# Batch 0's output in a fused attention and bilinear feed-forward kernel: two of three tile pairs by Strassen's products, with the sums that they need

## The chip, the cores and the metric

The kernel runs on one core of a Trainium2 chip. The metric is the device time of one execution in microseconds, start to finish; the time that counts is the median of several runs. Beside it stands one profiled execution, from which all rows below are taken. In the rows, PE is the matrix engine (TensorE) and PEld its loading of the stationary operand, DVE is VectorE, ACT is ScalarE, POOL is GpSimd, and SP is the engine that here only issues DMAs.

## The reference

For each of 4 batches and 8 heads (768 positions, head size 64), an 8 by 8 matrix `P` is normalised five times by rows and columns; `P` mixes the 8 blocks of `k` and `v`; block-wise attention follows; the heads are laid side by side into `x` (3072 rows of 512), and a bilinear feed-forward is applied:

```python
k_sorted = np.einsum('bhij,bhjcd->bhicd', P, k_b)      # and v_sorted likewise
scores   = scale * np.matmul(q_b, k_sb.transpose(0, 1, 2, 4, 3))
attn     = softmax(scores);  attn_out = np.matmul(attn, v_sb)
x = attn_out.transpose(0, 2, 1, 3).reshape(B * S, H * D)
out = ((x @ w_a) * (x @ w_b)) @ w_out                  # 512 -> 1536 -> 512
```

## The kernel before

**Order.** The order on all five engines is written out by hand: an instruction stands on its engine's queue where the program issues it, and each engine takes its queue from the front. Waits between engines are put in from the data and from the reuse of buffers.

**Feed-forward of one batch.** `ffn_ab(b, m, t)` is one step: for one of 12 feature tiles `m` and one half `t` of the batch's 768 positions (384 columns), PE forms `a` (4 products, L372) and `b` (4 products), ACT copies `a` from PSUM into `a_sb` (L402), and DVE multiplies it with `b` into `hT` (L403). Its PSUM tiles `pf` come from the pool `psF`, which has four buffers; so a step's `b` can start only when the multiplication two steps before has been done. A batch has 24 steps. The output follows, 6 chunks `c` of 128 rows:

- `ffn_out(b, c)`, in two parts: 12 products of 512 columns (L427) into one PSUM tile `po`, a copy into `o_sb` (ACT for even chunks, DVE for odd ones, by the helper at L175 and L177), and `store`, which issues the DMAs on SP (two for each chunk of batch 0, L414). Only batch 0 uses it.
- `ffn_out_pair(b, u)`, in four parts, used by batches 1 to 3: chunks `u` and `u + 3` together, as a 2 by 2 block product by Strassen's method, with seven products of 6 x 256 columns each (L481) in place of eight. It needs sums of blocks of the weights (`weight_sum`, L451, ten DVE instructions once per kernel, into `w_sums`) and sums of blocks of `hT` (`h_sums`, L472, twelve DVE instructions for each batch, four of which work in place in `hT`). ACT copies two products into `s` and two into the middle of the output tile (L495); DVE adds `y` twice (L519, L522) and writes two corners (L502).

Sums wait in a list, `sums_due`. `some_sums(n)` issues up to `n` of them at that place in DVE's order, and `sums_for` issues whatever is still needed before a product.

**Attention of the next batch**, in units between these steps (`interleave` with a list of places): for each of four head pairs `M` (mix, `pair_mix`: 12 products, L312, four copies out of two PSUM tiles, then transposing DMAs on SP), `R` (scores, 16 products L333, two exponentials on ACT, L338) and `O` (16 products L278, and on DVE a reciprocal and a multiplication for each half, L282 and L284, and one transposing DMA on SP into `xT`, L347). The PSUM tiles of `M`, `R` and `O` come from the pool `psA`, which has two buffers. In the rest of the text O1 is the `O` unit of the second head pair, and so on. Where batch 0 is computed, the units are those of batch 1: after the steps of `t = 1` with numbers 1, 2, 4, 5, 7, 9, 10, 12 come M0, M1, R0, M2, R1, M3, O0, R2, and after output parts 1, 3, 4, 6 (steps 13, 15, 16, 18) come O1, R3, O2, O3.

**Buffers.** The output tiles `o_sb` and `o2` share a tag of two buffers; `hT` and the sums `hs` have one buffer each. At the start of the program PE runs 46 products whose results nobody uses (`keep_busy`, L181, into `heat`).

Of the kernel before, what the change touches and what calls it, by code (L numbers as in the profile page):

```python
# [9 lines left out]
FP32 = mybir.dt.float32  # L10
# [13 lines left out]
def kernel(  # L24
# [12 lines left out]
    P = 128  # L37
    B, H, S, D = q.shape
# [134 lines left out]
    def copy(eng, out, in_):  # L173
        if eng == "act":
            nc.scalar.copy(out=out, in_=in_)  # L175
        else:
            nc.vector.tensor_copy(out=out, in_=in_)  # L177
# [200 lines left out]
        return hTs[b]  # L378

    sums_due = []  # L380

    def some_sums(n):
        for _ in range(min(n, len(sums_due))):
            sums_due.pop(0)[1]()
# [5 lines left out]
    def ffn_ab(b, m, t, begun=()):  # L390
        hT = hT_of(b)
        ab = []
        for n, w_sb in enumerate((w_a_sb, w_b_sb)):
            if n < len(begun):
                pf, k0 = begun[n], KA - 1
            else:
                pf, k0 = psF.tile([P, 512], FP32, tag="F", name="pf"), 0
            ab_mms(pf, w_sb, b, m, t, range(k0, KA))
            ab.append(pf)
            if n == 0:  # L400
                a_sb = ffp.tile([P, HW], BF16, tag="a_sb", name="a_sb", bufs=4)
                nc.scalar.copy(out=a_sb, in_=pf[:, 0:HW])  # L402
        nc.vector.tensor_mul(out=hT[:, m, t * HW:(t + 1) * HW], in0=a_sb,  # L403
                             in1=ab[1][:, 0:HW])
        if b > 0:
            if t == 1 and m >= KH and m != KH and m != KH + 2:
                sums_due[:0] = h_sums(b, *((m - KH - 1, 2) if m < KH + 4 else (m - KH, 1)))
            some_sums(1)

    def store(b, c, o):  # L410
        if b == 0:
# [10 lines left out]
    def ffn_out(b, c):  # L422
        v = {}

        def mms(ms):
            for m in ms:
                nc.tensor.matmul(v["po"], lhsT=hTs[b][:, m, c * P:(c + 1) * P],  # L427
                                 rhs=w_out_sb[:, m, :], start=(m == 0), stop=(m == KO - 1))

        def part1():  # L430
            v["po"] = psF.tile([P, DMODEL], FP32, tag="F", name="po")
            mms(range(KH))

        def part2():
            mms(range(KH, KO))
            o_sb = outp.tile([P, DMODEL], FP32, tag="o2", name="o_sb", bufs=2)
            copy("act" if c % 2 == 0 else "dve", o_sb, v["po"])
            store(b, c, o_sb)

        return [part1, part2]  # L440

# [14 lines left out]
        return hTs[b][:, c * KH + m, r * HW:(r + 1) * HW]  # L456

    def h_sums(b, m, nm):
        if b not in sums:
            sums[b] = ffp.tile([P, KH, 3, HW], BF16, tag="hs", name="hs")  # L460
        hT, hs = hTs[b], sums[b]

        def h(r, c, step):
            return _ap(hT, (c * KH + m) * S + r * HW,
                       [[KO * S, P], [S, nm]] + [[step, 2]] * (step is not None) + [[1, HW]])

        def s(i, k):
            return _ap(hs, (m * 3 + i) * HW,
                       [[KH * 3 * HW, P], [3 * HW, nm]] + [[HW, k]] * (k > 1) + [[1, HW]])

        turn = KH * S - HW
        return [("h", lambda to=to, x=x, y=y, op=op: nc.vector.tensor_tensor(  # L472
                    out=to, in0=x, in1=y, op=op))
                for to, x, y, op in (
                    (s(0, 2), h(0, 0, 0), h(0, 1, HW), ALU.add),
                    (s(2, 1), h(1, 0, None), h(1, 1, None), ALU.add),
                    (h(1, 0, turn), h(0, 0, KH * S + HW), h(1, 0, turn), ALU.subtract))]
# [10 lines left out]
    def ffn_out_pair(b, u):  # L488
        add3, add1, add2 = (lambda m, n=n: sums[b][:, m, n] for n in range(3))
        a11, a12, a21, a22 = (lambda m, r=r, c=c: h_part(b, r, c, m)  # L490
                              for r in range(2) for c in range(2))
        v = {}

        def keep(n, to):
            nc.scalar.copy(out=to, in_=v["ps"][n])  # L495

        def middle(n):
            return v["o"][:, n, (1 - n) * NH:(2 - n) * NH]

        def corner(n):  # L500
            to = v["o"][:, n, n * NH:(n + 1) * NH]
            nc.vector.tensor_tensor(out=to, in0=v["y"], in1=v["ps"][n], op=ALU.subtract)  # L502

        def part1():
            sums_for(1, 2)
            v["ps"] = [psF.tile([P, NH], FP32, tag="F", name="po") for _ in range(2)]
            v["s"] = outp.tile([P, 2, NH], FP32, tag="s", name="s")
            product(v["ps"][0], a11, w_sums[1], u)
            keep(0, v["s"][:, 0])
            product(v["ps"][1], a22, w_sums[2], u)  # L510
            keep(1, v["s"][:, 1])
            if b > 0:
                sums_for("h")

        def part2():
            sums_for("h", 0)
            v["y"] = outp.tile([P, NH], FP32, tag="y", name="y")
            v["o"] = outp.tile([P, 2, DMODEL], FP32, tag="o2", name="o2", bufs=2)
            nc.vector.tensor_tensor(out=v["y"], in0=v["s"][:, 0], in1=v["s"][:, 1], op=ALU.add)  # L519
            ps = psF.tile([P, NH], FP32, tag="F", name="po1")  # L520
            product(ps, add1, w_sums[0], u)
            nc.vector.tensor_tensor(out=v["y"], in0=ps, in1=v["y"], op=ALU.add)  # L522
            product(v["ps"][0], add3, B22, u, False)
            keep(0, middle(0))

        def part3():
            sums_for(3, 4)
            product(v["ps"][1], add2, B11, u, False)
            keep(1, middle(1))
            product(v["ps"][0], a12, w_sums[4], u, False)  # L530
            corner(0)

        def part4():
            store(b, u, v["o"][:, 0])
            product(v["ps"][1], a21, w_sums[3], u, False)
# [33 lines left out]
    def units_full(b):  # L569
        def M(g):  # L570
            pair_mix(g, 0, ("act", "act"))
            pair_mix(g, 1, ("act" if g >= 2 * HP else "dve", "act"))
            if g != 2 * HP - 1:
                turn_v(g)
            if g == 2 * HP + 1:
                hold(kvs[g % NBUF][0][0:1, 0, 0:1])
                load_pair(g + 2)
            if g in (HP + 1, HP + 3):
                spread(nc.gpsimd, p_col, (g - HP + 3) // 2 * 8, 8)
            if HP + 2 <= g + 1 < NPAIR and g + 1 != 2 * HP:  # L580
# [22 lines left out]
    with tc.manual_schedule(engines={ET.PE, ET.Pool, ET.SP, ET.Activation, ET.DVE}):  # L603
        if True:
# [14 lines left out]
                copy(eng, p_rep[:, hf * NR:(hf + 1) * NR],  # L619
                     _ap(p_fin, hf * NR, [[NB * NB, BH], [1, NR], [0, CG // 2]]))  # L620

            keep_busy(heat[:, 0], 46, P)
            for hp in range(HP):
                first_q(hp)
                if hp % 2:
# [114 lines left out]
        interleave(steps, units_half(), (2, 3, 3, 4, 4, 4, 5, 5, 6, 7, 7, 8, 9, 9, 10, 11))  # L740

        def outs(b):
            return [part for u in range(NCH // 2) for part in ffn_out_pair(b, u)]

        steps = [lambda m=m: ffn_ab(0, m, 1) for m in range(KO)]
        steps += [part for c in range(NCH) for part in ffn_out(0, c)]
        interleave(steps, units_full(1), (1, 2, 4, 5, 7, 9, 10, 12, 13, 15, 16, 18))

        halves = [n for m in range(KH) for n in (m, m + KH)]
        for b in range(1, B):  # L750
            steps = [lambda m=m, t=t, b=b: ffn_ab(b, m, t) for m in halves for t in range(2)]
            if b == 1:
                sums_due.extend(weight_sum(n, m, 3) for n in (1, 2, 0, 4, 3) for m in (0, 3))
            steps += outs(b)
            interleave(steps, units_full(b + 1) if b + 1 < B else [],
                       (1, 4, 8, 10, 13, 15, 17, 20, 21, 24, 25, 28))
# [30 lines left out]
```

## Time and profile before

| | |
|---|---|
| runs | 234.41, 234.69 and 236.04 us; median 234.69 us |
| profiled execution, its own time | 234.56 us |
| its span in the profile | 232.8 us |
| PE busy | 227.4 us (98%) |
| DVE busy | 141.6 us (61%) |
| ACT busy | 113.1 us (49%) |
| POOL busy | 68.7 us (30%) |
| granted TensorE clock | 1.00 |

Shares of the span are averages over stages, so the stage is what to read: batch 0's steps with `t = 1` run from about 41.1 to 62.7 us, its output from 62.7 to 80.3 us, batch 1's steps from there to 117.9 us and its output to 132.8 us. The time outside the span (234.56 - 232.8 = 1.76 us) lies around the profiled instructions.

### The profile page before, as it was taken

The page shows a single profiled execution, that of the slowest core. Times are in us where ns is not written, and L with a number is a line of the kernel's source. Part 1 is how long each engine was busy: PE and PEld are TensorE (multiplying, and loading weights), DVE is VectorE, ACT ScalarE, POOL GpSimd, SP SyncE. Part 2 cuts the span into 40 slices and gives each one's busy share as a digit, 9 for nine tenths or more (in the row PEclk, how much of TensorE's full clock was granted, in tenths as well). Part 3 has the DMA queues.
Part 4 walks back from the last instruction along what each step waited for, and adds up shares of the span by engine and source line. Part 5 has one row for each costly group of instructions (what it writes and reads, how often), then busy time and mean ns, then how long its engine had stood idle before and what let it go on. Part 6 is the DMA issues. An engine that isn't in the chain of part 4 may idle for free.

```text
span 232.8 us, 5674 instructions
## 1 busy us (share of the span) xinstructions
PE 227.4 (98%) x2259; PEld 156.6 (67%) x2259; DVE 141.6 (61%) x318; ACT 113.1 (49%) x237; POOL 68.7 (30%) x98
## 2 busy tenths in 40 slices
PE   7999999999999999999999999999999999999994
PEld 7776766766555465666689865666689865666883
DVE  7776677544645177768796334658786346576632
ACT  3575764577531165845552365755452333333331
POOL 8779839750035166325824000000000000000000
PEclk9999999999999999999999999999999999999999
DMA  5999999999779999996999757134016300000042
GB/s 74 201 201 199 207 203 200 152 179 186 136 113 200 229 169 200 137 130 95 161 155 209 148 133 95 23 59 75 8 37 157 148 32 4 0 0 3 3 170 99
DMA packets 54858, 28.68 MB, mean 123 GB/s; under 512 B 33712, under 2 KB 51888, under 8 KB 54832
## 3 DMA queue, kind: packets, MB, share of 16 engines
q0 software_dynamic: 18832, 14.16, 44.0%
q1 hardware_dynamic: 35856, 14.04, 34.0%
q8 instruction: 17, 0.28, 0.5%
q10 hardware_dynamic: 144, 0.13, 0.2%
q14 instruction: 9, 0.07, 0.1%
HBM read 28.32 MB, written 6.29 MB: 149 GB/s over the span
## 4 chain that ended last, share of the span: by engine, by line
PE 84%; DMA 11%; POOL 1%; issue 1%; DVE 1%; ACT 0%; SPq 0%; POOLq 0%; DVEq 0%
PE pf L372 53%; PE po L481 18%; DMA w_b_sb<-in_moe_w_b_dram 4%; PE mix L312 3%; PE o_ps L278 3%; DMA first<-in_q_dram 3%; DMA out_dram<-o_sb 2%; PE po L427 2%; PE sc L333 2%; DMA xT<-xp 2%; PE xt_ps L269 1%; PE vs_ps L254 1%; PE two L372 1%; PE sc L237 0%; DVE o_sb L177 0%
## 5 line engine op out<-in xcount | busy, mean ns | idle before, releaser
L403 DVE TENSOR_TENSOR hT<-a_sb,pf 128x384 bf16<-128x384 bf16 x96 | 52.9, 552 | 50.3 <-PE pf L372 27.1
L372 PE MATMUL pf<-xT,w_b_sb 128*128 128x384 bf16 x384 | 78.8, 326 | 0.2 <-DMA w_b_sb<-in_moe_w_b_dram 0.2
L372 PE MATMUL pf<-xT,w_a_sb 128*128 128x384 bf16 x376 | 77.1, 326 | 0.3 <-DMA xT<-xp 0.3
L402 ACT CAST a_sb<-pf 128x384 bf16<-128x384 f32 x94 | 45.4, 482 | 53.4 <-PE pf L372 34.5
L372 PEld LDWEIGHTS <-w_b_sb 128*128 128x128 bf16 x384 | 37.5, 98 | 25.8 <-issue 0.5
L372 PEld LDWEIGHTS <-w_a_sb 128*128 128x128 bf16 x384 | 35.3, 98 | 20.6
L481 PE MATMUL po<-w_sum,hT 128*128 128x256 bf16 x216 | 25.9, 273 | 0.0
L481 PEld LDWEIGHTS <-hT 128*128 128x128 bf16 x216 | 20.8, 98 | 2.6
L175 ACT CAST kv<-mix 128x384 bf16<-128x384 f32 x44 | 18.4, 490 | 5.7 <-PE mix L312 5.2
L338 ACT ACTIVATE eT<-sc 96x768 bf16<-96x768 f32 x24 | 18.0, 802 | 5.8 <-PE sc L333 5.8
L284 DVE TENSOR_TENSOR xp<-o_ps,rec 96x512 bf16<-96x512 f32 x24 | 16.5, 687 | 0.8
L481 PEld LDWEIGHTS <-hs 128*128 128x128 bf16 x162 | 15.7, 98 | 1.8
L427 PE MATMUL po<-w_out_sb,hT 128*128 128x512 bf16 x72 | 16.4, 379 | 0.0
L472 DVE TENSOR_TENSOR hs<-hT 128x768 bf16<-128x768 bf16 (+2 forms) x24 | 14.4, 610 | 0.4
L502 DVE TENSOR_TENSOR o<-y,po 128x256 f32<-128x256 f32 x18 | 7.6, 421 | 11.2 <-PE po L481 11.2
L299 POOL COPY qc<-q 128x384 uint32<-128x384 uint32 x12 | 6.9, 576 | 22.9 <-DMA q<-in_q_dram 13.1
L111 POOL COPY kvc<-kv 128x768 uint32<-128x768 uint32 x16 | 13.5, 852 | 0.1
L481 PE MATMUL po<-w_out_sb,hs 128*128 128x256 bf16 x108 | 13.3, 273 | 0.0
L495 ACT COPY s<-po 128x256 f32<-128x256 f32 x18 | 6.5, 374 | 13.4 <-PE po L481 13.4
L100 POOL DMA_DIRECT2D kv<-in_k_dram x16 | 11.7, 730 | 3.0 <-PE o_ps L278 2.1
L495 ACT COPY o<-po 128x256 f32<-128x256 f32 x18 | 6.7, 372 | 11.8 <-PE po L481 11.8
L100 POOL DMA_DIRECT2D kv<-in_v_dram x16 | 11.7, 729 | 2.2 <-DMA w_b_sb<-in_moe_w_b_dram 1.5
(83 smaller groups left out, 220.1 us busy)
## 6 DMA issues: line engine op xcount, KB each, us to landing
out_dram<-o SPq DMA_DIRECT2D x17, 256.0 KB, 2.1
kv<-in_k_dram POOLq DMA_DIRECT2D x16, 192.0 KB, 7.0
kv<-in_v_dram POOLq DMA_DIRECT2D x16, 192.0 KB, 7.6
q<-in_q_dram POOLq DMA_DIRECT2D x12, 192.0 KB, 7.7
w_out_sb<-in_moe_w_out_dram POOLq DMA_DIRECT2D x3, 512.0 KB, 13.6
out_dram<-o_sb SPq DMA_DIRECT2D x12, 128.0 KB, 5.1
w_a_sb<-in_moe_w_a_dram POOLq DMA_DIRECT2D x2, 512.0 KB, 11.4
w_b_sb<-in_moe_w_b_dram POOLq DMA_DIRECT2D x2, 512.0 KB, 13.0
```

The source lines that it names most:

```text
L100: nc.gpsimd.dma_start(out=to, in_=_ap(t, base, [[W, P], [S * D, 2], [1, W]]))
L111: nc.gpsimd.tensor_copy(out=to.bitcast(U32).rearrange("p c n d -> p n c d"), in_=loaded[g][0].bitcast(U32).rearrange("p n (c d) -> p n c d ...
L175: nc.scalar.copy(out=out, in_=in_)
L284: nc.vector.tensor_tensor(out=_ap(xp, i0 * 2 * D, [[nxp * 2 * D, BLK], [D, 2], [2 * D, NBH], [1, D]]), in0=_ap(o_ps, 1, [[1024, BLK], [511 ...
L338: nc.scalar.activation(out=eT[:, hf, :, 0:HB], in_=sc[0:BLK, :, 0:HB], func=AF.Exp, scale=float(scale))
L372: nc.tensor.matmul(pf[:, 0:HW], lhsT=w_sb[:, kc, m * P:(m + 1) * P], rhs=x_cols(b, kc, t), start=(kc == 0), stop=(kc == KA - 1))
L402: nc.scalar.copy(out=a_sb, in_=pf[:, 0:HW])
L403: nc.vector.tensor_mul(out=hT[:, m, t * HW:(t + 1) * HW], in0=a_sb, in1=ab[1][:, 0:HW])
L427: nc.tensor.matmul(v["po"], lhsT=hTs[b][:, m, c * P:(c + 1) * P], rhs=w_out_sb[:, m, :], start=(m == 0), stop=(m == KO - 1))
L472: return [("h", lambda to=to, x=x, y=y, op=op: nc.vector.tensor_tensor(out=to, in0=x, in1=y, op=op)) for to, x, y, op in ((s(0, 2), h(0, 0 ...
L481: nc.tensor.matmul(to, lhsT=lhs(m)[:, u * P:(u + 1) * P], rhs=rhs[:, m], start=start and m == 0, stop=(m == KH - 1), skip_group_check=not ...
L495: nc.scalar.copy(out=to, in_=v["ps"][n])
```

## The change

- Batch 0's output: chunks 0 and 3 stay with `ffn_out`; the pairs (1, 4) and (2, 5) go through `ffn_out_pair`. The number of parts stays twelve, so the places of the units stay as they are.
- The weight sums move from the start of batch 1 to step 9 of batch 0's steps with `t = 1`; batch 0 gets sums of `hT` too, over the 256 of 384 columns that the two pairs use. `PACE` says how many sums each step of `t = 1` issues. The feature tiles of these steps are taken in the order 0, 6, 1, 7, and so on, as in the other batches.
- In every batch, `some_sums` now stands ahead of the step's multiplication and not behind it. The two parts of `ffn_out` issue two sums each.
- The copies of `ffn_out` go all to ACT, and so do the copies of batch 1's `pair_mix`, of which DVE had one in four.
- Output tiles have three buffers; `keep_busy` at the start issues 52 products.

```diff
     sums_due = []
+    PACE = (1,1,1,1,1,1,1,1,2,3,3,3)
...
+        some_sums(1 if b else t * PACE[2 * (m % KH) + m // KH])
         nc.vector.tensor_mul(out=hT[:, m, t * HW:(t + 1) * HW], in0=a_sb,
                              in1=ab[1][:, 0:HW])
-        if b > 0:
-            if t == 1 and m >= KH and m != KH and m != KH + 2:
-                sums_due[:0] = h_sums(b, *((m - KH - 1, 2) if m < KH + 4 else (m - KH, 1)))
-            some_sums(1)
+        if t == 1 and m >= KH and m != KH and m != KH + 2:
+            sums_due[:0] = h_sums(b, *((m - KH - 1, 2) if m < KH + 4 else (m - KH, 1)))
...
         def part1():
             v["po"] = psF.tile([P, DMODEL], FP32, tag="F", name="po")
             mms(range(KH))
+            some_sums(2)
 
         def part2():
             mms(range(KH, KO))
-            o_sb = outp.tile([P, DMODEL], FP32, tag="o2", name="o_sb", bufs=2)
-            copy("act" if c % 2 == 0 else "dve", o_sb, v["po"])
+            o_sb = outp.tile([P, DMODEL], FP32, tag="o2", name="o_sb", bufs=3)
+            copy("act", o_sb, v["po"])
             store(b, c, o_sb)
+            some_sums(2)
...
     def h_sums(b, m, nm):
+        n0, n = (P, HW - P) if b == 0 else (0, HW)
...
-            v["o"] = outp.tile([P, 2, DMODEL], FP32, tag="o2", name="o2", bufs=2)
+            v["o"] = outp.tile([P, 2, DMODEL], FP32, tag="o2", name="o2", bufs=3)
...
-            pair_mix(g, 1, ("act" if g >= 2 * HP else "dve", "act"))
+            pair_mix(g, 1, ("act", "act"))
...
-            keep_busy(heat[:, 0], 46, P)
+            keep_busy(heat[:, 0], 52, P)
...
         def outs(b):
-            return [part for u in range(NCH // 2) for part in ffn_out_pair(b, u)]
-
-        steps = [lambda m=m: ffn_ab(0, m, 1) for m in range(KO)]
-        steps += [part for c in range(NCH) for part in ffn_out(0, c)]
+            plain = (0,) if b == 0 else ()
+            return ([part for u in plain for c in (u, u + 3) for part in ffn_out(b, c)]
+                    + [part for u in range(NCH // 2) if u not in plain
+                       for part in ffn_out_pair(b, u)])
+
+        halves = [n for m in range(KH) for n in (m, m + KH)]
+        steps = [lambda m=m: ffn_ab(0, m, 1) for m in halves]
+        steps[8] = lambda m=halves[8]: (
+            sums_due.extend(weight_sum(n, m0, 3) for n in (1, 2, 0, 4, 3) for m0 in range(0, KH, 3)),
+            ffn_ab(0, m, 1))
+        steps += outs(0)
         interleave(steps, units_full(1), (1, 2, 4, 5, 7, 9, 10, 12, 13, 15, 16, 18))
...
-            if b == 1:
-                sums_due.extend(weight_sum(n, m, 3) for n in (1, 2, 0, 4, 3) for m in (0, 3))
```

More of the change, by code (lines that the diff above doesn't have):

```diff
@@ L463, in h @@
         def h(r, c, step):
-            return _ap(hT, (c * KH + m) * S + r * HW,
-                       [[KO * S, P], [S, nm]] + [[step, 2]] * (step is not None) + [[1, HW]])
+            return _ap(hT, (c * KH + m) * S + r * HW + n0,
+                       [[KO * S, P], [S, nm]] + [[step, 2]] * (step is not None) + [[1, n]])
         def s(i, k):
-            return _ap(hs, (m * 3 + i) * HW,
-                       [[KH * 3 * HW, P], [3 * HW, nm]] + [[HW, k]] * (k > 1) + [[1, HW]])
+            return _ap(hs, (m * 3 + i) * HW + n0,
+                       [[KH * 3 * HW, P], [3 * HW, nm]] + [[HW, k]] * (k > 1) + [[1, n]])
         turn = KH * S - HW
@@ L742, in outs @@
         def outs(b):
-            return [part for u in range(NCH // 2) for part in ffn_out_pair(b, u)]
-        steps = [lambda m=m: ffn_ab(0, m, 1) for m in range(KO)]
-        steps += [part for c in range(NCH) for part in ffn_out(0, c)]
+            plain = (0,) if b == 0 else ()
[8 more added lines that the diff above has]
+        steps += outs(0)
         interleave(steps, units_full(1), (1, 2, 4, 5, 7, 9, 10, 12, 13, 15, 16, 18))
-        halves = [n for m in range(KH) for n in (m, m + KH)]
         for b in range(1, B):
             steps = [lambda m=m, t=t, b=b: ffn_ab(b, m, t) for m in halves for t in range(2)]
-            if b == 1:
-                sums_due.extend(weight_sum(n, m, 3) for n in (1, 2, 0, 4, 3) for m in (0, 3))
             steps += outs(b)
```

## The prediction, on record before the changed kernel ran

> **What bounds the kernel now.** I read the windows by stage first, then PE's timeline, the chain of waits, and DVE's timeline last. The windows (stretch, length, busy us and instruction count of PE, PEld, DVE, ACT, POOL, granted clock, DMA share, GB/s) for batch 0's second half of steps, its output, and batch 1's steps:
>
> ```profile
> 41.13:62.70 21.57, 21.57 (x217) 14.10 (x215) 11.10 (x23) 14.04 (x30) 7.42 (x8) 1.00 1.38 167
> 62.70:81.25 18.55, 18.23 (x144) 9.10 (x141) 6.64 (x15) 4.69 (x7) 5.92 (x10) 1.00 1.10 173
> 81.25:117.93 36.68, 36.68 (x334) 23.35 (x334) 27.95 (x52) 21.92 (x47) 20.14 (x30) 1.00 1.13 148
> ```
>
> PE is busy in all of it but 0.32 us of batch 0's output; DVE and ACT have room everywhere. So time is won only by taking work from PE or by closing that gap, and lost wherever DVE's queue gets so late that PE waits. PE's timeline gives the price of a product and the gap:
>
> ```profile
> 67.17 0.51 PE L333 MATMUL sc<-qTf,kv 64*128 64x96 bf16 x16
> ...
> 72.51 7.93 PE L427 MATMUL po<-w_out_sb,hT 128*128 128x512 bf16 x36
> 80.28 0.65 PE L372 MATMUL pf<-xT,w_a_sb 128*128 128x384 bf16 x3
> 81.25 0.32 PE L372 MATMUL pf<-xT,w_a_sb 128*128 128x384 bf16 x1 [0.32 <-DMA xT<-xp]
> ```
>
> From start to next start, 36 plain products take 80.28 - 72.51 = 7.77 us, 0.2158 each. The chain of waits (start, us) has the same for Strassen's products, and what the gap hangs on:
>
> ```profile
> 70.36 5.42 DMA out_dram<-o_sb
> ...
> 76.26 4.94 DMA xT<-xp
> ...
> 123.61 9.17 PE po L481 x84
> ```
>
> 84 products of 256 columns take 9.17 us, 0.1092 each. The gap: O3's `xT` stood on SP behind a store whose copy waited for an output buffer; it was issued at 76.26 and landed 4.94 later.
>
> **The change, part by part.**
>
> *Products.* Two pairs: 2 x 24 x 0.2158 = 10.36 us go, 2 x 42 x 0.1092 = 9.17 come: -1.19 us, all on PE's path.
>
> [...]
>
> *The gap.* Eight products of a step take 1.30 us in the chain, so the fourth should have started at 80.28 + 3 x 0.1625 = 80.77; it started at 81.25. With three buffers and copies on ACT, no store waits for a buffer ahead of O3's `xT`. If DVE has O3 done in time (below), -0.48 us.
>
> *DVE.* Into the first two windows come ten weight sums, twelve `h_sums`, and for two pairs four corners and four additions of `y`; four copies of `mix` and three of `o_sb` leave. Prices are distances from start to next start in DVE's timeline (a duration overlaps the next instruction by some 0.08):
>
> ```profile
> 56.31 0.56 DVE L403 TENSOR_TENSOR hT<-a_sb,pf 128x384 bf16<-128x384 bf16 x1 [1.56 <-ACT a_sb L402]
> ...
> 64.68 0.69 DVE L284 TENSOR_TENSOR xp<-o_ps,rec 96x512 bf16<-96x512 f32 x1
> ...
> 89.71 0.55 DVE L451 TENSOR_TENSOR w_sum<-w_out_sb 128x768 bf16<-128x768 bf16 x1
> ...
> 90.67 1.44 DVE L451 TENSOR_TENSOR w_sum<-w_out_sb 128x768 bf16<-128x768 bf16 x1
> ...
> 93.54 0.96 DVE L472 TENSOR_TENSOR hs<-hT 128x1536 bf16<-128x1536 bf16 x1
> ...
> 95.39 0.55 DVE L472 TENSOR_TENSOR hs<-hT 128x768 bf16<-128x768 bf16 x1
> ```
>
> A multiplication (`mul`) or a weight sum occupies 0.47; an `O` unit's four instructions 1.67 (O0 ran from 59.91 to the next start at 61.58). The last two rows give `h_sums` 0.52 ns an element beyond a constant, so 1024, 512 and 256 elements, which no row shows, take 0.61, 0.34 and 0.20. In all 4.70 + 4.88 = 9.6 us of sums, where DVE idles 10.47 + 11.91; what matters is when. By steps of `t = 1`:
>
> - step 8's `mul` starts at 56.31 as before; a dependency of 0.1 and two `h_sums` (0.95) follow; step 9's `mul` 57.8 to 58.3
> - one `h_sum`, two weight sums (1.55); step 10's `mul` 59.85 to 60.3 (start before: 59.44)
> - O0 to 62.0, three `h_sums` (0.88); step 11's `mul` 62.9 to 63.35 (before 61.58)
> - three weight sums (1.41); step 12's `mul` 64.8 to 65.2 (before 62.42)
> - 0.1 and two `h_sums` (0.54), then O1 from 65.9 to 67.6 (its end before: 66.1)
> - one `h_sum`, five weight sums to 70.25; O2 to 71.9; `y` twice to 72.8; O3 to 74.55
>
> Who waits? PE's step 12 needs step 10's `mul` for its `b` at 61.5: done at 60.4. The products of chunk 3 at 65.8 and 67.9 need those of steps 11 and 12: done. R3 is caught: its two score tiles reuse the `psA` tiles of O1, it starts at 67.17, its second half 0.22 later, and O1 ends at 67.6: **PE stalls about 0.3 us**. Were every sum 0.60, as the mean of before's weight sums (677 ns less the overlap) makes them, the thirteen sums ahead of O1 add 13 x 0.13 = 1.7: a stall of 2.0. Were they free, there is none. I take 0.3: POOL, beside whose copy (90.84 to 91.69) the 1.44 row ran, has no copy between 49.9 and 75.0.
>
> [...]
>
> The weight sums also wait for the third load of `w_out`, issued at 40.8 with 16.2 to landing: 57.0, 1.9 us ahead of need. Behind a late one queue step 10's `mul`, O0, and PE by `psF`.
>
> *DMAs.* On SP, four stores of chunks 0 and 3 stand ahead of O2's `xT`, their copies on ACT done by 69.8, and four stores took 2.51: out of the way by 72. O3's `xT`, ready at 74.55, is issued 1.7 us earlier than before and with 4.94 lands at 79.5; PE needs it at 80.77 - 1.19 + 0.33 = 79.9. The gap closes, by 0.4. The other eight stores come behind it, no later than before's six (79.1 on). POOL's loads for batch 2 wait for O0's and O1's `xT`, up to 1.5 us later, and are needed after 82.
>
> *ACT.* Four copies of `mix` in a row took 1.63 us in batch 1. After M3 they end near 59.25, and O0's second half needs the tile at 59.30: I add 0.03 (bounds 0 and 0.3, the price of one copy less what fits). ACT idles 7.5 us in the first window, which hides the other M units; without that, `a_sb` and `mul` would be late by up to 0.4. Copies of `o_sb` lie in ACT's waits for PE.
>
> *Sums ahead of the multiplication.* The same instructions, in the time in which `mul` waits for PE (27.1 us in all); a PSUM tile has 1.95 us of PE until its reuse, the longest sum occupies 0.88: nothing (without that cover, up to 0.9 for each). Behind a batch's last `mul` the order is the same. Batch 1 loses ten sums from DVE: no gain, since PE never idles there.
>
> *52 products at the start.* The ten ahead of the second reciprocal's product cost 0.067 each, so six cost 0.40; PE waited 0.19 there for `q`. The 0.21 left runs into PE's wait of 0.15 for `w_b` at 20.13. I add 0.06; bounds 0 and 0.28 (at 4.75 / 46 = 0.103 each).
>
> *Sum.* -1.19 - 0.48 + 0.30 + 0.03 + 0.06 = **-1.28 us**. The profiled execution (234.56: span 232.8 and 1.76 around it, which stays) would take 233.3; the median lies 0.13 above it, so 234.69 - 1.28 = **233.4 us**.
>
> **The rivals.**
>
> *DVE's queue becomes the bound in batch 0's output.* Place: O1's `xp`, and R3 behind it. For it: thirteen sums now stand ahead of O1, and weight sums of before took up to 1.44. Against it: POOL is quiet. Price at 0.60 a sum: R3 waits 1.7 more, and O3's `xT` comes 18 x 0.13 = 2.3 later, at 81.8, against a need of 81.6: -1.28 + 1.7 + 0.2 = +0.6, **235.3 us**. Slower than before from the point where DVE is 1.3 us later at O1 than worked out.
>
> *The transpose sets the end of the stage anyway.* If O3's `xT` lands at 81.20 again, PE's fourth product starts at 81.25 as before and all that was won is waited away: **234.7 us**. For it: landings of this row run from 2.8 to 10.7 us. Against it: it would need 6.6 us where it took 4.94 from a busier queue.
>
> *No stall at all:* -1.19 - 0.48 = -1.67: **233.0 us**. For it: O1 misses R3 by only 0.3.
>
> **How the numbers follow.** Forecast 0.58, DVE 0.16, transpose 0.12, no stall 0.14. The range, 232.5 to 235.3, reaches from the no-stall case less half a microsecond for the spread of the runs up to the DVE rival, so that its dearer half and little else is left out. A change of 1% (2.35 us) is about what a measurement of this kernel can tell from none. Faster than 232.3 takes more than products, gap and start can give: 0.06. Slower than 237.0 needs DVE 3.6 us later at O1 than worked out: 0.08. Within: 0.86.
>
> **What would show it.** Right: 84 products of 256 columns near 70 us take 9.17; step 12's `mul` starts near 64.8; PE idles 0.2 to 0.4 at R3, released by DVE; batch 1's first step shows no wait for `xT`; DVE's busy time in batch 1's steps falls by some 5 us and PE's does not change. Wrong: weight sums over 0.6 in their new place, PE idle for over 1 us between 57 and 80 us, DVE waiting for a `w_out` load, or PE for `xT` near 80 us.

## The result, and the profile after

The changed kernel took 240.57 us, median of four runs (240.31 to 241.49), against 234.69 before: a ratio of 1.025, 95% interval 1.022 to 1.028. It is 5.9 us slower where 1.3 us less was forecast, and outside the range. The profiled execution took 240.4 us, its span 238.6. (Its mean granted clock of 0.993 is no disturbance of the run: the stretch that lowers it is shown below.)

The windows by stage of the changed kernel, cut where the same work begins and ends (columns as in the windows before: length; busy us and count of PE, PEld, DVE, ACT, POOL; clock; DMA share; GB/s):

```profile
42.41:63.98 21.57, 21.57 (x217) 14.10 (x215) 13.83 (x28) 15.17 (x34) 7.42 (x8) 1.00 1.39 160
63.98:85.60 21.62, 17.37 (x179) 12.63 (x176) 14.09 (x34) 7.09 (x14) 7.22 (x10) 1.00 1.09 141
85.60:123.81 38.21, 38.21 (x334) 24.26 (x334) 22.39 (x41) 21.93 (x47) 21.59 (x30) 0.96 1.05 150
```

The first stage is as long as before, 21.57 us, but starts 1.28 later. The second, from the output's first product to the fourth product of batch 1's first step, grew from 18.55 to 21.62: PE is busy 0.86 us less and idle 4.25 us where it was idle 0.32. The third, batch 1's steps, grew from 36.68 to 38.21 at a granted clock of 0.96. In the second, PE's timeline shows where:

```profile
69.07 0.34 PE L333 MATMUL sc<-qTf,kv 64*128 64x96 bf16 x8 [0.27 <-DVE xp L284]
...
71.14 1.47 PE L484 MATMUL po<-w_sum,hT 128*128 128x256 bf16 x12
...
80.81 0.49 PE L372 MATMUL pf<-xT,w_a_sb 128*128 128x384 bf16 x2
83.80 0.32 PE L372 MATMUL pf<-xT,w_a_sb 128*128 128x384 bf16 x1 [2.50 <-DMA xT<-xp]
85.60 0.48 PE L372 MATMUL pf<-xT,w_a_sb 128*128 128x384 bf16 x1 [1.49 <-DMA xT<-xp]
```

0.27 us is the stall at R3; 2.50 and 1.49 are waits for O2's and O3's `xT`, 3.99 us together. What follows is in the chain of waits, before and then after:

```profile
81.25 0.97 PE pf L372 x5
82.22 0.67 PE mix L312 x12
82.89 3.94 PE pf L372 x24
86.83 0.67 PE mix L312 x12
```

```profile
76.00 9.56 DMA xT<-xp
85.56 0.04 issue
85.60 1.76 PE pf L372 x5
87.36 1.28 PE mix L312 x12
88.64 4.06 PE pf L372 x24
92.70 0.67 PE mix L312 x12
```

O3's `xT` was issued at 76.00, 0.26 earlier than before, and took 9.56 us in place of 4.94. Behind the wait five products took 1.76 and twelve of `mix` 1.28, where before they took 0.97 and 0.67. The windows give the reason, in the clock (third column from the end):

```profile
84.00:86.00 2.00, 0.51 (x3) 0.22 (x2) 0.00 (x0) 0.00 (x0) 0.18 (x1) 0.86 1.28 256
86.00:88.00 2.00, 2.00 (x13) 1.31 (x12) 0.53 (x1) 0.48 (x1) 1.86 (x3) 0.50 1.04 377
88.00:90.00 2.00, 2.00 (x16) 1.37 (x14) 0.02 (x1) 1.96 (x5) 1.56 (x3) 0.79 1.05 139
```

Full (1.00) in the 16 us before, the clock was half (0.50) after PE's pause and back at full by 90 (1.00 from 90 to 92). From the fourth product to the second `mix` unit, before takes 86.83 - 81.25 = 5.58 us, after 92.70 - 85.60 = 7.10, 1.52 more. So the span's 5.8 us are 1.28 at the start, 21.62 - 18.55 = 3.07 in the output, and 1.5 of slower clock; from there on the distance between the kernels stays the same within 0.1.

What changed around the transfers into `xT`? POOL's timeline, before:

```profile
67.19 0.18 POOL L295 COPY held<-xT 1x1 bf16<-1x1 bf16 x1 [17.34 <-DMA xT<-xp]
67.31 0.76 POOL L100 DMA_DIRECT2D kv<-in_k_dram  x1
...
71.48 0.18 POOL L295 COPY held<-xT 1x1 bf16<-1x1 bf16 x1 [1.97 <-DMA xT<-xp]
71.94 0.72 POOL L100 DMA_DIRECT2D kv<-in_k_dram  x1 [0.28 <-issue]
```

and after:

```profile
69.87 1.40 POOL L295 COPY held<-xT 1x1 bf16<-1x1 bf16 x1 [17.66 <-DMA xT<-xp]
71.21 0.77 POOL L100 DMA_DIRECT2D kv<-in_k_dram  x1
...
73.40 0.34 POOL L295 COPY held<-xT 1x1 bf16<-1x1 bf16 x1
73.68 0.72 POOL L100 DMA_DIRECT2D kv<-in_k_dram  x1
```

A one-element copy (`hold`, into `held`) waits for O0's `xT` and lets pair 8's three loads (576 KB) go; a second one waits for O1's and lets pair 9's go. Before, the two groups start 4.6 us apart and the first is under way when O2's `xT` is issued (71.51). After, the first copy starts late and takes 1.40 us, and the second group follows the first without a pause, so that O2's and O3's `xT`, issued at 73.39 and 76.00, meet both: the last load of pair 8 landed at 79.9 and that of pair 9 at 85.0, where before they landed at 75.0 and 79.8.

### The profile page after: what moved, and what is told of

Same layout as the page of the kernel before. It is cut to its first block, busy times and chain, and to the rows that moved or that the text cites. A ratio compares the mean times of both kernels' runs of the same rounds, so it can differ in the third digit from the quotient of the medians.

```text
span 238.6 us, 5782 instructions
## 1 busy us (share of the span) xinstructions
PE 229.1 (96%) x2301; PEld 161.9 (68%) x2301; DVE 146.5 (61%) x331; ACT 116.9 (49%) x248; POOL 71.4 (30%) x98
## 4 chain that ended last, share of the span: by engine, by line
PE 82%; DMA 8%; DVE 5%; POOL 2%; issue 1%; ACT 1%; POOLq 0%; DVEq 0%
PE pf L372 50%; PE po L484 19%; DMA kv<-in_k_dram 4%; DMA xT<-xp 4%; PE mix L312 3%; PE o_ps L278 3%; PE sc L333 2%; POOL kv L100 1%; DVE xp L284 1%; DVE w_sum L453 1%; DVE hT L405 1%; DVE hs L475 1%; PE sc L237 1%; PE xt_ps L269 1%; POOL first L93 1%
## 5 line engine op out<-in xcount | busy, mean ns | idle before, releaser
L484 PE MATMUL po<-w_sum,hT 128*128 128x256 bf16 x264 | 31.6, 273 | 0.0
L484 PEld LDWEIGHTS <-hT 128*128 128x128 bf16 x264 | 25.4, 98 | 3.2
L484 PEld LDWEIGHTS <-hs 128*128 128x128 bf16 x198 | 19.2, 98 | 2.2
L475 DVE TENSOR_TENSOR hs<-hT 128x768 bf16<-128x768 bf16 (+5 forms) x32 | 19.2, 616 | 0.5
L505 DVE TENSOR_TENSOR o<-y,po 128x256 f32<-128x256 f32 x22 | 9.3, 421 | 12.7 <-PE po L484 12.6
L484 PE MATMUL po<-w_out_sb,hs 128*128 128x256 bf16 x132 | 16.4, 273 | 0.0
L498 ACT COPY s<-po 128x256 f32<-128x256 f32 x22 | 8.0, 374 | 16.1 <-PE po L484 16.1
L498 ACT COPY o<-po 128x256 f32<-128x256 f32 x22 | 8.2, 373 | 14.7 <-PE po L484 14.7
L111 POOL COPY kvc<-kv 128x768 uint32<-128x768 uint32 x16 | 14.8, 934 | 0.1
L278 PEld LDWEIGHTS <-eT 96*128 96x128 bf16 x256 | 10.3, 97 | 1.7
## 6 DMA issues: line engine op xcount, KB each, us to landing
w_a_sb<-in_moe_w_a_dram POOLq DMA_DIRECT2D x2, 512.0 KB, 10.9
```

Of the source, the lines that this page charges most:

```text
L111: nc.gpsimd.tensor_copy(out=to.bitcast(U32).rearrange("p c n d -> p n c d"), in_=loaded[g][0].bitcast(U32).rearrange("p n (c d) -> p n c d ...
L278: nc.tensor.matmul(o_ps[:, e, i * (D + 1):(i + 1) * (D + 1)], lhsT=eT[:, hf, e, i * BLK:i * BLK + P], rhs=vs[0:BLK, i0 + i, V0 - 1 + e * ( ...
L484: nc.tensor.matmul(to, lhsT=lhs(m)[:, u * P:(u + 1) * P], rhs=rhs[:, m], start=start and m == 0, stop=(m == KH - 1), skip_group_check=not ...
```

## The experiments

The theory after the two profiles: the loads of pairs 8 and 9 meet the last two transfers into `xT`, and POOL's held-up copy pushes them together. Its rivals: DVE's new order, ACT's copies, the buffers or the start cost the time, or two transposing DMAs issued 2.6 us apart slow each other without any loads. Times are medians. The groups of experiments ran on different chips, each with the kernel before beside it.

**52 products, or 46.** Two kernels: the changed one with `keep_busy(heat[:, 0], 46, P)`, and the kernel before with 52.

> The changed kernel with 46 unused products at the start, as before. In its profile PE began its first product of w_b at 21.41 us where before it was 20.13, 1.28 us later. Theory S1 (the six further products push the start): 239.3 us, and that product back near 20.1. Rival S2 (the start depends on when the second load of q lands, 9.75 us against 8.52, whatever PE does): unchanged, 240.6 us.

> The kernel before with 52 unused products at the start instead of 46. S1 (they push the start): 235.0 to 236.0 us, first product of w_b at 20.5 to 21.4 us. S2 (landing of q): no change, 234.7 us.

The kernel before with 52 took 235.27 us, a ratio to before of 1.002 (0.999 to 1.005), and its first `w_b` product came at 19.82, no later than the 20.13 of 46. So the 52 products cost nothing in the kernel before, and the 1.28 us at the start were a late landing of `first` in that execution (7.3 us after its issue, against 6.1 before): the product came at 20.52 and 19.84 in two others of the same kernel. The changed kernel with 46 gave two groups, eight executions from 233.04 to 235.02 and two near 240.5. The first group lies some 0.9 us under the kernel before on that chip (235.28), which is near the forecast. The profiled one was of the second, with the same picture: POOL's copy took 2.56 us, O3's `xT` 9.99. The profile of the kernel before with 52 shows a milder form by chance, with none of the change's other edits: O0's `xT` landed late (POOL's copy behind it ran at 68.12, before at 67.19), the two groups of loads went 2.3 us apart (68.24 and 70.54), O2's and O3's `xT` took 8.4 and 7.3 us, and PE waited 1.43.

**The loads released elsewhere.** In the changed kernel, pairs 8 and 9 wait for M3's copy and not for `xT`:

```diff
-            hold(xT_of(1)[0:1, g % HP, 0:1])
+            hold(kvs[(2 * HP - 1) % NBUF][0][0:1, 0, 0:1] if g < HP + 2
+                 else xT_of(1)[0:1, g % HP, 0:1])
```

> The changed kernel, with the loads of k, v and q for batch 2's first two pairs released by M3's copies (about 60.5 us) and no longer by the landing of O0's and O1's xT (69.9 us and later). Theory T1 (these six loads, issued in one run from 71.2 to 75.8 us, keep the DMA engines while O2's and O3's xT are in flight, so that these take 10.4 and 9.6 us instead of 6.4 and 4.9): both land within some 6 us, PE waits under 0.5 us at batch 1's first step, its clock stays at 1.00, and the time falls by some 5.5 to 6 us, to about 235. Rival T2 (two transposes issued 2.6 us apart with no store between slow each other): unchanged, 240.6 us. Rival T3 (DVE's lateness at O0 to O3 is what costs): unchanged.

236.43 us, from 233.75 to 239.21. In its profile the waits for `xT` at batch 1's first step are gone, but the loads, now over 10 us earlier, fly with `qTf`; the chain:

```profile
59.70 10.27 DMA qTf<-qc
69.97 0.14 issue
70.10 0.52 PE sc L333 x16
```

PE waited 2.74 us for it. The loads now meet this transposing DMA (10.27 us) and O0's `xT` (10.3): the collision moved. O2's and O3's `xT`, again issued 2.6 us apart (76.2 and 78.8) but now with no loads beside them, took 3.1 and 2.8. So these two, as close together as in the changed kernel, did not slow each other by themselves.

**Three buffers and ACT copies alone**, put into the kernel before:

```diff
-            o_sb = outp.tile([P, DMODEL], FP32, tag="o2", name="o_sb", bufs=2)
-            copy("act" if c % 2 == 0 else "dve", o_sb, v["po"])
+            o_sb = outp.tile([P, DMODEL], FP32, tag="o2", name="o_sb", bufs=3)
+            copy("act", o_sb, v["po"])
```

> The kernel before with three output buffers and all copies of batch 0's plain output on ACT; no Strassen products in batch 0, no sums moved. As predicted for this part alone: O3's xT is issued near 74.7 us and lands near 79.7, no gap at batch 1's first step, 234.2 us. T1: it comes nearer to the loads of the second pair (71.9 to 74.1 us), lands with 6 us or a little more, and the time is 234.2 to 234.8. T2 (transposes issued close together slow each other): O2's and O3's xT take some 10 us, PE waits 3 us or more, 238 us or more.

234.29 us, ratio 0.996 (0.994 to 0.997): a small gain. O3's `xT` was issued at 74.28, 2 us earlier, and took 6.97, so PE still waited 0.34. An earlier issue into the same traffic bought a longer flight (6.97 us against 4.94). Where the gain comes from is not shown: the profile's span, 232.8 us, is that of the first profile of the kernel before. No other kernel here that computes the whole reference has a gain this safe.

**Without transposing DMAs.** All 48 became plain copies, in both kernels:

> The kernel before with each of its 48 transposing DMAs on SP replaced by plain copies of about as many bytes between the same tiles (two copies where the partitions differ, one for qTf). The elements are not transposed, so this leaves out that part of the computation; all engines' instructions and all loads stay. It is the yardstick for the next kernel. Expected: xT lands 2 to 4 us after its issue instead of 5 to 7, no wait for xT at batch 1's first step, 232 to 235 us.

> The changed kernel with the same replacement of its 48 transposing DMAs by plain copies. Theory (the change's arithmetic does what was forecast, and the loss lies in the flight of the last two transposing DMAs beside the loads): with these DMAs gone the change is worth what its products and its stall at R3 make, -1.19 and +0.30, so 0.5 to 1.5 us less than the yardstick; no idle time of several us at batch 1's first step, no lower clock behind it. Rival (DVE's new order, the ACT copies or three buffers make the loss): still 2 us or more above the yardstick. A plain copy that is itself late beside the loads would leave a part of the loss: then between the two. On POOL, the one-element copy out of xT still takes 1 to 2.5 us beside DVE's sums.

Before 234.18, after 233.40 us: the change gains 0.78. All twelve executions of the changed form lie between 233.20 and 234.34. The chain at batch 1's first step has no wait and no slow products:

```profile
79.65 1.30 PE pf L374 x8
80.95 0.67 PE mix L312 x12
```

The kernel before has no wait for `xT` in this form, so the sum without its gap term, -1.19 + 0.30 + 0.03 + 0.06 = -0.80, is what to compare, and it holds. The loss sits in the flight of these DMAs and not in the order on DVE, ACT's copies or the buffers by themselves. These copies, though, are fast (2.2 to 4.8 us into `xT` there), so they also release the loads early, at 64.9 and 72.4. With POOL's copy replaced by a write:

```diff
-            hold(xT_of(1)[0:1, g % HP, 0:1])
+            nc.gpsimd.memset(xp[0:1, 0, 0, 0:1], 0.0)
```

> The last kernel with POOL's one-element copy out of xT, which holds back the loads of pairs 8, 9 and 10, replaced by a write of 0 to one element of that pair's xp, which waits until the copy into xT has read it. Theory (POOL's copy is held up while DVE runs sums of two inputs): the write takes at most 0.3 us where the copy takes 1 to 2.5, and pair 8's loads start that much earlier. Rival (the one-element copy is long for another reason, such as POOL's own clearing up behind the spread): the write is as long. The time differs from the last kernel's by under 0.5 us, since plain copies do not make TensorE wait.

233.70 us, the same. The write took 0.09 us, but there was nothing to win: the copy in the kernel before this one took 0.18 to 0.50. It says nothing of a held-up copy.

**The two disputed costs by themselves.**

> A kernel of its own that leaves out the whole computation and measures two disputed costs by themselves. First: runs of 8 two-input sums (128x768 bf16) and of 12 one-input copies on DVE, and beside each run a one-element copy or a one-element write on POOL, released when the run's first instruction is done. Theory: the copy beside two-input sums ends only about when the run ends (2 to 3.5 us), the write takes under 0.3 us in all; beside one-input copies, either is possible, since no run shows it. Rival: all four take 0.2 us. Second: eight stretches of 140 products of 512 columns (about 30 us each), between them pauses of TensorE of about 0.5 to 12 us. Theory: the granted clock behind a pause of 4 us or more is about half for 2 to 4 us, as in the changed kernel (0.50 and 0.79 in two windows of 2 us), and full behind a pause under 1 us. Rival (the low clock in that kernel has another cause): full behind every pause.

DVE's copies went ahead of TensorE, which never paused (one row of products from 19.70 to 254.69 us), the clock stayed at 1.00, and that half showed nothing. One sample each on POOL: the copy took 0.45 beside the sums, the write 0.09; the copy meant for the one-input copies ran beside the same sums (at 11.09) and took 0.44, and the write beside one-input copies took 2.93. Against the theory; so again, six times and in a forced order:

> The measurement of the two disputed costs again, leaving out the reference's whole computation, with an order that the dependencies force (in the kernel before it DVE's copies went ahead, so that TensorE never paused). Six rounds of four runs on DVE: 8 two-input sums or 12 one-input copies, each with a one-element copy or a one-element write on POOL, released by the run's first instruction. Theory from the single samples of the last kernel (0.45 and 0.09 beside sums, 2.93 for the write beside copies): beside sums the copy takes 0.2 to 0.5 in most rounds and now and then 1 to 2.5, which is what the changed kernel showed; beside one-input copies both last about as long as the run, 3 us. Rival: the copy beside sums is always under 0.5, and the 1.40 and 2.56 had another cause. Then nine stretches of 100 products (some 22 us each), with pauses of about 0.7, 1.8, 3, 3.5, 4, 5, 7 and 9 us between them. Theory: full clock behind the short pauses, about half for 2 to 4 us behind those from 3 or 4 us on. Rival: full behind all.

POOL's timeline, first two rounds (`el_two`: copy beside sums; then write beside sums; `el_one`: copy beside one-input copies; then write):

```profile
12.10 0.44 POOL L74 COPY el_two<-d 1x1 bf16<-1x1 bf16 x1 [10.01 <-DVE d L69]
15.84 0.09 POOL L76 MEMSET d<- 1x1 bf16 x1 [3.30 <-DVE d L69]
19.39 2.66 POOL L74 COPY el_one<-d 1x1 bf16<-1x1 bf16 x1 [3.46 <-DVE d L71]
22.50 0.24 POOL L76 MEMSET d<- 1x1 bf16 x1 [0.45 <-DVE d L71]
25.92 3.25 POOL L74 COPY el_two<-d 1x1 bf16<-1x1 bf16 x1 [3.18 <-DVE d L69]
29.83 0.09 POOL L76 MEMSET d<- 1x1 bf16 x1 [0.65 <-DVE d L69]
```

The later rounds repeat the second: 3.26 for the copy, 0.09 for the write. In five of six rounds a one-element copy on POOL ended only with DVE's run of eight sums (25.92 + 3.25 = 29.17; DVE's sixteen sums from 25.31 on took 7.74, so the eighth ended near 29.2); the write took 0.09 in all six. Why the one lasts and the other does not is not shown: beside one-input copies the copy took 2.66 to 2.93 as well, and the write 0.24. With the measurement beside sums, 1.40 us of `held` beside five sums (2.42), and 2.56 beside these and one more, fit: in each of these two profiles the copy ended some 0.4 us before the run did, when its last sum had begun. PE's pauses, from its timeline:

```profile
144.55 21.76 PE L86 MATMUL acc<-rhs,wt 128*128 128x512 bf16 x100 [1.63 <-DVE rhs L92]
169.13 23.45 PE L86 MATMUL acc<-rhs,wt 128*128 128x512 bf16 x100 [2.82 <-DVE rhs L92]
195.99 23.44 PE L86 MATMUL acc<-rhs,wt 128*128 128x512 bf16 x100 [3.42 <-DVE rhs L92]
```

Behind a pause of 1.63 us the next 100 products took as long as behind one of 0.44 (21.76 and 21.74 us); behind one of 2.82 they took 23.45 - 21.76 = 1.7 us longer, and behind longer ones about as much (1.3 to 2.3 up to 9.36 us). Behind the pause of 3.42 the granted clock was 0.70 from 196 to 198 us, 0.50 to 200, 0.95 to 202 and 1.00 after. The 1.5 us of slow clock in the changed kernel, behind waits of 2.50 and 1.49, is a price of this size.

**The changed kernel again.**

> The changed kernel as it is, more often and on another day's chip. Theory (the collision of loads and transposing DMAs depends on when transfers land): two groups of times, about 233.5 to 235 and about 240, as with 46 products. Rival (with 52 products the collision is there in every execution): all near 240.

> The changed kernel once more, for a profile of one of its executions near 233 us, of which the last run had one in six. Theory: in such an execution pair 8's loads start before POOL's copy is caught by DVE's run of five sums (near 69), or O2's and O3's xT land 5 to 7 us after their issue; PE waits under 1 us at batch 1's first step and the clock stays at full. Rival: the same landings as in the slow executions, and the difference lies elsewhere, at the start or in the last batches.

Of twelve executions, eleven took 239.91 to 241.63 us, and one 232.96. With the first four that is one near 233 in sixteen. Both profiles are of executions near 240, with O3's `xT` in flight for 10.62 and 10.88 us. The first product of `w_b` came at 19.84 in the second, without a late start; there the clock stayed at half from about 84.5 to 91 (0.58, 0.50, 0.50 and 0.71 in the windows of 2 us from 84 to 92), and its price was 2.7 us and not 1.5. There is no profile of an execution near 233, only one of a related kernel, below. The kernel before has executions in this region too: of the 138 that ran beside the experiments, twelve took 237.59 to 241.11 us at a mean granted clock of 0.986 or 0.993, as these do. None of them was profiled, so that it is the same collision is a guess; the change would then have made a rare event the usual one.

**Slower copies.** The 48 DMAs became copies in pieces of 128 bytes, meant as a stand-in with a longer flight:

> The kernel before with its 48 transposing DMAs replaced by copies in pieces of 128 bytes (the elements are not transposed, which leaves out that part of the computation). The pieces are meant to make the copies slower in flight than the plain copies (1.9 to 5.5 us for xT), nearer to the transposing DMAs (2.8 to 10.7). The yardstick for the next two: 233.5 to 235 us.

> The changed kernel with the same copies in pieces. Theory (slow DMAs beside two pairs' loads, which POOL's held copy lets go in one run): with slower copies a part of the executions shows a wait of PE at batch 1's first step and a time of 236 to 240; where no copy is late, 0.5 to 1.5 us under the yardstick. Rival (only transposing DMAs are made late by the loads): 0.5 to 1.5 us under the yardstick in all executions, as with plain copies.

> The last kernel with POOL's copy out of xT replaced by the write to xp, which DVE's sums do not hold up (0.09 and 0.24 us in the measurement by itself). Theory that POOL's wait decides: fewer or no executions over 236. Rival (the wait has no part in it): the same times as the last kernel.

Before 234.87, after 237.29 (234.89 to 238.68), with the write 236.30 us (236.06 to 239.53). The loss is back in part, so it doesn't take transposing DMAs: transfers with a longer flight were enough (into `xT` 3.0 us in the median and up to 9.5 in the write's profile, against 2.3 and up to 5.5 in that of the changed kernel with plain copies); and replacing POOL's copy does not remove it. In the write's profile SP issued O0's transfer into `xT` at 65.20, it took some 4 us, and the write ran only at 69.46; pair 8's loads went at 69.92 and pair 9's at 72.14, in one run again. My theory that POOL's held-up copy decides fell here: it adds to the delay, but the landings are close enough without it.

**The loads themselves.** Pair 9's loads left out (its work uses pair 8's data), in both kernels; and the kernel before with pair 8's loads put beside pair 9's:

```diff
-            load_pair(2 * HP + (g - HP + 1) // 2)
+            if g == HP + 1:
+                loaded[2 * HP + 1] = loaded[2 * HP]
+            else:
+                load_pair(2 * HP + (g - HP + 1) // 2)
```

> The kernel before with copies in pieces, and without the loads of pair 9: its work uses pair 8's data, which leaves 576 KB of loads out of the stretch before batch 1's first step. The yardstick for the next kernel; on its own expected at 234 to 235, since the transfers into xT make TensorE wait by only 0.3 us there.

> The changed kernel with copies in pieces, and without the loads of pair 9. Theory (the last two transfers into xT are late because two pairs' loads fly with them): the loss goes, 0.5 to 1.5 us under the yardstick, no group near 238, PE's wait at batch 1's first step under 0.5 us. Rival (O2's and O3's transfers are late for another reason, such as SP's queue, which issues them late): as with all loads, 236 to 238.

> The kernel before with copies in pieces and one thing moved: pair 8's loads wait for O1's transfer into xT instead of O0's, so that the loads of pairs 8 and 9 go in one run. Theory (loads in one run beside the last two transfers are enough): both pairs' loads from about 70 to 74.5, O3's xT 6 to 9 us in flight, PE waits 1 to 3 us at batch 1's first step, 236 to 239. Rival (it takes the change's later sums as well): 234.5 to 235.5.

Without pair 9's loads: before 234.44, after 233.93 us (233.26 to 234.35). The change gains 0.5 again and the group near 238 is gone, although POOL's copy took 1.83 us in the profile and pair 8's loads went at 70.03. Its chain:

```profile
75.48 4.84 DMA xT<-xp
80.36 0.97 PE pf L380 x5
81.34 0.67 PE mix L313 x12
```

And the kernel before with both groups in one run took 236.08 us, against 234.87 with copies in pieces alone, on another chip. Each beside the unchanged kernel before on its own chip, the ratios are 1.004 (1.002 to 1.007) and 0.998 (0.996 to 1.001): 1.2 to 1.4 us lost with none of the change in it. O3's `xT` with the copies in pieces alone, then with the loads in one run, and PE's wait for it there:

```profile
77.62 3.57 DMA xT<-xp
```

```profile
76.75 5.52 DMA xT<-xp
```

```profile
82.32 0.34 PE L380 MATMUL pf<-xT,w_a_sb 128*128 128x384 bf16 x1 [1.21 <-DMA xT<-xp]
```

The distance between the groups changed little (3.1 us, then 2.2); what changed more is their time, 2 to 3 us later (69.62 and 71.80, against 66.77 and 69.90). So the loads of two pairs beside the last two transfers are what costs; in the kernel before they cost about half of what they cost in the changed one (2.4). That PE needs `xT` later in the kernel before would explain the half, and was not tested.

**Which edit pushes them together?** The copies of `mix` back on DVE as before:

```diff
-            pair_mix(g, 1, ("act", "act"))
+            pair_mix(g, 1, ("act" if g >= 2 * HP else "dve", "act"))
```

> The changed kernel with copies in pieces, and with one edit undone: the first half of each second mixing of batch 1 is copied by DVE again and not by ACT. Theory (ACT's four copies in a row, 1.63 us against 1.41, make SP issue the transfers into vs and then O0's into xT some 0.5 us later, and with it pair 8's loads): 235 to 236.5, fewer executions at a lower clock. Rival (this edit has no part): 236.5 to 238 as with it.

237.93 us (235.09 to 238.73): undoing that edit does not remove the loss. The profiled execution took 238.33 us. POOL's timeline and, below it, the chain:

```profile
68.04 2.22 POOL L295 COPY held<-xT 1x1 bf16<-1x1 bf16 x1 [15.92 <-DMA xT<-xp]
70.20 0.76 POOL L100 DMA_DIRECT2D kv<-in_k_dram  x1
...
72.67 0.72 POOL L100 DMA_DIRECT2D kv<-in_k_dram  x1
```

```profile
75.65 7.47 DMA xT<-xp
83.16 1.75 PE pf L377 x5
84.90 1.28 PE mix L313 x12
```

The changed kernel with pieces, whose profiled execution was its fastest (234.89), shows the other group:

```profile
66.61 0.18 POOL L295 COPY held<-xT 1x1 bf16<-1x1 bf16 x1 [13.85 <-DMA xT<-xp]
66.73 0.76 POOL L100 DMA_DIRECT2D kv<-in_k_dram  x1
...
74.33 0.18 POOL L295 COPY held<-xT 1x1 bf16<-1x1 bf16 x1 [5.41 <-DMA xT<-xp]
74.78 0.71 POOL L100 DMA_DIRECT2D kv<-in_k_dram  x1 [0.27 <-issue]
```

Here O0's `xT` landed before DVE's run of sums began, the two groups of loads start 8 us apart, O3's `xT` took 5.63 us, and PE waited 0.87. The two kernels differ by the edit undone, but both have executions of both kinds.

## Why the prediction was wrong, by its steps

- *Products*: right. From 71.14 to 80.81, less 0.49 for an `O` unit between, 84 products took 9.18 us (9.17 forecast). Without late transfers the whole change gave 0.5 to 0.8 of the 1.28 us.
- *DVE's schedule and R3*: right. Less the 1.28 of the start, step 12's `mul` began at 64.86 (64.8), five sums took 2.42 us, 0.47 each, and the stall was 0.27 (0.30). One ground for it was misread: POOL does have copies between 49.9 and 75.0, the one-element copies into `held` at 67.19 and 71.48. The price held because it was the copy that waited (1.40 us), not the sums. The rival "DVE's queue becomes the bound" did not happen. DVE's busy time in batch 1's window fell by 5.6 us (some 5 forecast).
- *The gap*: the step that failed. It took O3's flight, 4.94 us, as a property of the DMA and moved it 1.7 us earlier. Issued near the time worked out (76.00 less 1.28, against 74.55), it took 9.56; O2's, which the step did not cost at all, made PE wait 2.50 by itself. PE waiting for `xT` near 80 us was the last of the prediction's own signs of being wrong. In place of -0.48 stood +3.7 of waiting, and 1.5 of slower clock behind it.
- *POOL's loads*: the sentence that they come up to 1.5 us later and are needed after 82 was the place to stop. Pair 8's came 3.9 us later, 2.6 without the start, and they were asked only whether they would be in time, not what they would fly beside. The kernels without pair 9's loads show that this is the cause for the copies in pieces; for the transposing DMAs the release at M3 points the same way (2.8 and 3.1 us of flight without loads, 9.6 and 10.4 with them). That a copy on POOL and DVE's sums may hold each other up was weighed for the sums and not for the copy; it costs 1 to 2.5 us of the delay (the copy took 1.03 to 2.56 in the four profiles near 240 us and 0.18 in the one before), but the kernel with the write lost time without it.
- *The rival "the transpose sets the end of the stage anyway"* named the right row and the wrong price. It quoted landings of up to 10.7 us, yet priced only a landing at 81.20 again, which is what three buffers alone gave in the kernel before (74.28 + 6.97 = 81.25). With 10.7 from 74.55, `xT` lands at 85.25 against a need of 79.9: 233.4 + 5.3 = 238.7, and with the 1.7 us of the clock 240.4. That this meets the measured time is partly chance, since 1.28 us of the profiled execution came from its late start. A landing later than before's was never given a chance.
- *The clock*: no term. From its first product on, PE's longest wait in the profile before is 0.32 us, at a granted clock of 1.00, so nothing in it shows the price of a wait of several us; a rival with such a wait needed it, and would have had to call it unknown. In the measurement by itself a pause of 2.82 us cost 1.7 more.
- *52 products*: 0.06 forecast; none to be seen in two profiled executions with them in which the loads came in time (first `w_b` product at 19.82 and 19.84), 1.28 in the one with the late load of `first`.

What stays open is why the landings fall so in fifteen of sixteen executions of the changed kernel, against two of ten with 46 products. No record puts the two on the same chip, so the six products, or the chip, may be what tips it. O0's `xT` is issued behind a full queue on SP (one transposing DMA after another from 60.90 to 66.17 in the changed kernel's profile), and the moment from which POOL can go on differs by some 3 us between executions of alike kernels (66.61, 68.04 and 69.46 with pieces). ACT's copies and POOL's held copy were each tried as the trigger, and neither is it alone. DVE's sums and the later O2 weren't tried apart. With the transposing DMAs themselves only the release at M3, the number of products at the start and the buffers were varied; the loads in one run, the write and the missing loads were measured with copies alone.

## What to carry to other kernels

A flight time read from one profile belongs to the traffic that it was read in: for every DMA that a change moves, list what will be in flight beside it, above all bulk loads that a moved event releases. Price the longest landing that the profile shows, not only the usual one, and if PE would then wait as long as where products slowed here (1.87 and 0.52 us in a row were enough, 1.63 were not), add the clock's price, 1.5 to 2.7 us in the changed kernel's profiles. And look for what paces background loads: here a one-element copy, which took 1.03 to 2.56 us beside sums on another engine and 0.18 without them.

## What the runs showed of the hardware

- The last two transposing DMAs into `xT` before batch 1's first step (192 KB each) took 9.0 to 10.9 us from issue to landing, beside the loads of two pairs (1.15 MB), in the four profiles near 240 us of the changed kernel, one of them with 46 products; with the release at M3, `qTf` and O0's `xT`, which met these loads, took 10.3. In the kernel before the last two took 6.4 and 4.9, and the median over all twelve into `xT` was 3.9 (2.8 to 10.7).
- A one-element copy on POOL took 0.18 us at 67.19 in the kernel before, while DVE did nothing, and 3.25 or 3.26 beside eight two-input sums in a row on DVE in five of six rounds, where it ended with the run (0.44 in the first). A write took 0.09 beside the same sums. Beside one-input copies of 128x768 the copy took 2.66 to 2.93, and a write 0.24 in six rounds but 2.93 in the earlier measurement.
- Behind a pause of TensorE of 1.63 us, 100 products took as long as behind one of 0.44 (21.76 and 21.74 us); behind pauses of 2.82 to 9.36 they took 1.3 to 2.3 us longer, and behind that of 3.42 the granted clock was 0.50 to 0.70 for 4 us. In the kernels, four products took 1.48 or 1.49 us in place of 0.81 behind waits of 2.34 and 0.19 us in a row and of 1.87 and 0.52, and 0.81 behind one of 1.43; behind one of 2.74 the clock was 0.85, 0.50 and 0.80 in windows of 2 us, and behind 1.35 and 3.95 in a row it stayed at half for over 6 us (0.58, 0.50, 0.50, 0.71).
